# Two rows of w2 moved to the front of the down projection, in three transfers issued by GpSimd and one by SP

## The chip, the core and the metric

The kernel runs on one core of one Trainium2 chip. The metric is the device time of one execution in microseconds; lower is better. Three runs of the kernel before took 138.73, 138.76 and 138.94 us, so the median is 138.76 us. A profile shows one execution, whose span is counted from the first to the last instruction; what lies around the span belongs to the time as well.

## The reference

One decode step of a transformer block for a batch of 4, in bfloat16:

```
h   = x + attention(layernorm(x)) @ wo          # 32 heads, 4 kv heads, last 2048 keys
g   = layernorm(h) @ w1                         # [4,1024] @ [1024,3584]
u   = layernorm(h) @ w3
out = h + (silu(g) * u) @ w2                    # [4,3584] @ [3584,1024]
```

Some 55.6 MB of weights and caches are read once each: wq and wo (8 MB each), the windows of K and V (8 MB each), w1, w3 and w2 (7 MB each).

## The kernel before

**Storage.** One tile in SBUF, `ring`, has five units of 32 KB per partition. wq, K, V, wo, w1, w3 and w2 are laid into the units one after another, and each transfer waits until the readers of what it overwrites are done. w1 takes unit 1 and most of unit 2, w3 unit 3 and most of unit 4.

**w2.** It is cut into 128 partitions with 28 rows of 1024 values each (2 KB per row and partition), so partition p holds rows 28p to 28p+27. `W2B = [13, 8, 4, 2, 1]` gives the pieces: the first 13 rows of every partition go to the start of the ring (unit 0), the others one behind another to the start of unit 1, where w1 lies. The piece of 1 row is loaded as two halves (`h` in the loop at L509 to L512).

**Transfers.** `load` (L124) issues on the queue of SP. All the large transfers go through it, in the order of the code: wq in two pieces, K, V, wo, w1, w3, then w2 in pieces of 13, 8, 4, 2, 1/2 and 1/2 rows. In one queue the transfers of a DMA engine follow each other in order. x is loaded from the queue of ACT at the start. GpSimd issues no transfer.

**The stage around the change.** The order of the instructions is written out by hand (`manual_schedule`). After attention and the output projection, layernorm gives `hn_T`. `up_projection` (L489) multiplies it by w1 into `gate` (64 matmuls, in two halves of 8 steps of 4), ACT and DVE compute silu from it, and the second `up_projection` multiplies by w3 into `up`. DVE forms `hg` from both in two halves and transposes each into `hg_T` (L520, L218), which holds 28 columns of 32, one for each row of w2.

**The down projection** is in two forms. The first 21 rows, of the pieces 13 and 8 (`NE = 2`), are "early": two matmuls of 512 columns for each row, into `early_ps` (L538). DVE then adds `early_ps` to `h1`, the residual, in two steps of 64 partitions (L549). The other 7 rows, of the pieces 4, 2 and 1, are "late": six matmuls for each row (four of 128 columns, two of 256) into three tiles `y2_ps` (L554). Behind the piece of 4, one matmul with an identity (L565) adds a part of `h1` into `y2_ps[1]`. At the end ACT and DVE write `res` (L577 to L582) and SP and ACT issue four output transfers (L587).

On PE the order before is: up projection, early 13 rows, early 8 rows, late 4 rows, the `h1` matmul, late 2 rows, late 1 row. PE waits ahead of each piece for its transfer.

Of the kernel before, what the change touches and what calls it, by code (L numbers as in the profile page):

```python
# [10 lines left out]
P = 128  # L11
# [10 lines left out]
def kernel(  # L22
# [20 lines left out]
    nc = tc.nc  # L43

    B, _, D = A_x.shape
# [7 lines left out]
    FC = F // P  # L53
    NK = W // P
    C = 4
    R = 32
    S = R // B
    DQ = D // C
# [23 lines left out]
    w2_v = B_w2.rearrange("(p fc) n -> p fc n", fc=FC)  # L82
# [15 lines left out]
    def at(unit, *shape):  # L98
        o = unit * UNIT
        view = ring[:, o : o + int(np.prod(shape))]  # L100
        if len(shape) == 1:
            return view
        names = "abc"[: len(shape)]
        return view.rearrange(
            f"p ({' '.join(names)}) -> p {' '.join(names)}", **dict(zip(names, shape))
        )
# [4 lines left out]
    wo_s = at(3, T, D)  # L111
    w1_s = at(1, KC, F)
    w3_s = at(3, KC, F)
    W2B = [13, 8, 4, 2, 1]
    w2_s = []
    o = 0
    for i, n in enumerate(W2B):
        if i == 1:
            o = UNIT
# [3 lines left out]
    def load(dst, src):  # L123
        nc.sync.dma_start(out=dst, in_=src)  # L124
# [13 lines left out]
    for b in range(B):  # L138
# [10 lines left out]
    ident_f = const.tile([P, P], FP32)  # L149
# [8 lines left out]
        out=same[:], in_=t32[:].rearrange("p (o h) -> p o h", o=1).to_broadcast([P, C, R])  # L158
    )
    gmask = const.tile([P, 1, Hkv], BF16)  # L160
    with nc.allow_low_precision("sums of zeros and a single one"):
        nc.vector.tensor_reduce(
            out=gmask[:, 0], in_=t32[:].rearrange("p (g r) -> p g r", g=Hkv), axis=AX.X, op=ALU.add
# [3 lines left out]
    for j in range(JM):  # L167
# [3 lines left out]
        out=nscale[:], in_=ident_f[:2, :2], scalar=-qscale, op=ALU.mult  # L171
# [5 lines left out]
        out=place[:, : R * C].rearrange("p (h e) -> p h e", e=C)[:, :, C - 1], in_=t32[:]  # L177
# [6 lines left out]
        out=gather[:, :, :B], in_=ident[:].rearrange("p (c b s) -> p c b s", c=C, b=B)[:, :, :, 0]  # L184
# [44 lines left out]
    for kc in range(KC):  # L229
        for hf in range(2):  # L230
            for c in range(C):
                o = (2 * c + hf) * HALF * Dh
                nc.tensor.matmul(  # L233
                    q_ps[R * c : R * c + R, hf],
                    lhsT=xn_T[:, kc, :],
                    rhs=wq_s[:, kc, o : o + HALF * Dh],
                    start=(kc == 0),
                    stop=(kc == KC - 1),
                    tile_position=(0, R * c),
# [5 lines left out]
    for r in range(REP):  # L245
# [8 lines left out]
        out=Qm[:].rearrange("p b (g y) -> p b g y", y=QW)[:, :, :, :REP],  # L254
        in_=qT_ps[:, :, :, :B].rearrange("p r g b -> p b g r"),
# [184 lines left out]
    for e in range(C):  # L440
        nc.tensor.matmul(
            on_ps[:],
            lhsT=place[:, C - 1 - e : C - 1 - e + P],
            rhs=om[:, :, e * T : (e + 1) * T],
            start=(e == 0),
            stop=(e == C - 1),
# [6 lines left out]
    for i in range(2):  # L453
        for k in range(2):
            c = i + 2 * k
            nc.tensor.matmul(
                y_ps[R * i : R * i + R, k],
                lhsT=gather[:, c, :],
                rhs=x_nat[:],
                start=(k == 0),  # L460
                stop=False,
                tile_position=(0, R * i),
                skip_group_check=True,
            )
    for t in range(T):
        row = wo_s[:, t].rearrange("p (k i n) -> p i k n", k=2, i=2)
        for i in range(2):
            nc.tensor.matmul(  # L468
                y_ps[R * i : R * i + R],
                lhsT=oP[:, t, :],  # L470
                rhs=row[:, i],
                start=False,
                stop=(t == T - 1),
                tile_position=(0, R * i),
                skip_group_check=True,
            )
    load(w3_s, w3_v)
    load(w2_s[0], w2_v[:, : W2B[0], :])
    h1 = act.tile([P, DQ], FP32)
# [9 lines left out]
    def up_projection(w, out_ps):  # L489
        cols = w.rearrange("p k (c q h j) -> p k c h q j", c=C, h=2, j=FJ)  # L490
        for hf in range(2):
            for kc in range(KC):
                for c in range(C):
                    nc.tensor.matmul(  # L494
                        out_ps[hf][R * c : R * c + R, :],
                        lhsT=hn_T[:, kc, :],
                        rhs=cols[:, kc, c, hf],
                        start=(kc == 0),
                        stop=(kc == KC - 1),
                        tile_position=(0, R * c),  # L500
                    )
# [4 lines left out]
    hg = act.tile([P, 2, FH], BF16, tag="hg")  # L506
    up_projection(w1_s, [gate_ps[:, hf, :FH] for hf in range(2)])
    fc = W2B[0]
    for w, n in zip(w2_s[1:], W2B[1:]):  # L509
        for h in (slice(0, D),) if n > 1 else (slice(0, D // 2), slice(D // 2, D)):  # L510
            load(w[:, :, h], w2_v[:, fc : fc + n, h])
        fc += n  # L512
    nc.scalar.activation(out=eg[:], in_=gate_ps[:, :, :FH], func=ACT.Exp, scale=-1.0)
    nc.scalar.activation(out=eg[:], in_=eg[:], func=ACT.Identity, bias=1.0)  # L514
# [3 lines left out]
    hg_T = act.tile([P, FC, R], BF16)  # L518
    for hf in range(2):
# [5 lines left out]
    DH = DQ // 2  # L525
    y2_ps = [
        ps.tile(shape, FP32, tag=tag, name="y2_ps")
        for shape, tag in (([P, DH], "scA"), ([P, DH], "ktB"), ([P, DQ], "scB"))
    ]
    NE = 2  # L530
    FE = sum(W2B[:NE])

    fc = 0
    for w, n in zip(w2_s[:NE], W2B[:NE]):
        for ff in range(n):
            row = w[:, ff].rearrange("p (k i n) -> p i k n", k=2, i=2)
            for i in range(2):
                nc.tensor.matmul(  # L538
                    early_ps[R * i : R * i + R],
                    lhsT=hg_T[:, fc, :],  # L540
                    rhs=row[:, i],
                    start=(fc == 0),
                    stop=(fc == FE - 1),
                    tile_position=(0, R * i),
                )
            fc += 1
    for k in range(2):
        part = h1[2 * R * k : 2 * R * k + 2 * R, :]
        nc.vector.tensor_tensor(out=part, in0=early_ps[:, k], in1=part, op=ALU.add)  # L549
    for m, (w, n) in enumerate(zip(w2_s[NE:], W2B[NE:])):  # L550
        for ff in range(n):
            for t, c, size in ((0, 0, DH), (0, 1, DH), (1, 0, DH), (1, 1, DH), (2, 2, DQ), (2, 3, DQ)):
                o = c * DQ + t % 2 * DH
                nc.tensor.matmul(  # L554
                    y2_ps[t][R * c : R * c + R, :],
                    lhsT=hg_T[:, fc, :],
                    rhs=w[:, ff, o : o + size],
                    start=(fc == FE),
                    stop=(fc == FC - 1),
                    tile_position=(0, R * c),  # L560
                    skip_group_check=True,
                )
            fc += 1
        if m == 0:
            nc.tensor.matmul(  # L565
                y2_ps[1][: 2 * R, :],
                lhsT=ident_f[:, : 2 * R],
                rhs=h1[:, DH:],
                start=False,
                stop=False,  # L570
                skip_group_check=True,
            )
    res = act.tile([P, DQ], BF16)
    for k in range(2):
        part = slice(2 * R * k, 2 * R * k + 2 * R)
        if k == 0:
            nc.scalar.copy(out=res[part, DH:], in_=y2_ps[1][part, :])  # L577
            nc.vector.tensor_tensor(
                out=res[part, :DH], in0=y2_ps[0][part, :], in1=h1[part, :DH], op=ALU.add
            )  # L580
        else:
            nc.vector.tensor_tensor(  # L582
                out=res[part, :], in0=y2_ps[2][part, :], in1=h1[part, :], op=ALU.add
            )
        for i, eng in enumerate((nc.sync, nc.scalar)):
            c = 2 * k + i
            eng.dma_start(  # L587
                out=out_flat[:, c * DQ : (c + 1) * DQ], in_=res[R * c : R * c + B, :]
# [31 lines left out]
```

## Time and profile before

| | before |
|---|---|
| median of 3 runs | 138.76 us |
| the profiled execution's own time | 138.7 us |
| its span | 136.7 us |
| PE busy, DVE busy, ACT busy, POOL busy | 74.8, 49.9, 28.8, 15.3 us |
| read from HBM, mean rate over the span | 55.58 MB, 407 GB/s |
| last matmul of the gate ends | 104.1 us |
| up projection (w3) | 116.3 to 121.1 us |
| early matmuls of 13 rows, of 8 rows | 124.35 to 127.3, 129.15 to 131.05 us |
| last matmul ends | 133.95 us |

The page of the profile gives busy time by engine, the span in 40 slices, the DMA queues, and the chain that ended last. From the trace come, besides, the order in time of all instructions, and of every DMA packet its queue, start, duration and bytes. The packets do not name their DMA engine; but on an engine a packet starts as the one before it ends, so that the sixteen series ("lanes") can mostly be followed. Each transfer ends on each lane that it uses with a packet of 4 bytes, which signals its end. An instruction that waits for a transfer waits for the signals of all its lanes.

### The profile page before, as it was taken

How to read it: one execution, taken by the hardware profiler on the slowest of the kernel's cores; microseconds unless marked ns; L12 is line 12 of the kernel's file. 1: busy time of each engine (PE TensorE's matmuls, PEld its weight loads, DVE VectorE, ACT ScalarE, POOL GpSimd, SP SyncE). 2: the span in 40 equal slices, each digit the busy share in tenths (PEclk: the TensorE clock that was granted, in tenths of full speed). 3: DMA queues.
4: the chain of work that ended last, by engine and by line, in shares of the span. 5: the costliest groups of instructions: out<-in, count | busy, mean ns of one | idle time of the engine just before them, and what ended most of it. 6: DMA issues, size and time to landing. Idle time of an engine off the chain costs nothing.

```text
span 136.7 us, 1762 instructions
## 1 busy us (share of the span) xinstructions
PE 74.8 (55%) x762; PEld 40.6 (30%) x762; DVE 49.9 (37%) x50; ACT 28.8 (21%) x32; POOL 15.3 (11%) x41
## 2 busy tenths in 40 slices
PE   0000044959999986029966875994184000946471
PEld 0000011439957852014423323341042000413240
DVE  0000110006526363989799920004100594090022
ACT  3000130025968495104000000000405400000000
POOL 7300060000000000000176333000200000000000
PEclk9999999999999999955999999599959955599999
DMA  4999697999999999998978979969799798999960
GB/s 163 497 454 538 269 537 307 432 417 451 408 432 436 412 436 408 436 585 360 556 326 364 556 326 475 520 285 537 336 470 508 302 520 372 384 423 432 384 245 2
DMA packets 2795, 55.70 MB, mean 408 GB/s; under 512 B 324, under 2 KB 612, under 8 KB 740
## 3 DMA queue, kind: packets, MB, share of 16 engines
q1 hardware_dynamic: 2752, 55.58, 95.3%
q8 instruction: 6, 0.10, 0.3%
q10 hardware_dynamic: 36, 0.01, 0.0%
q14 instruction: 1, 0.01, 0.0%
HBM read 55.58 MB, written 0.01 MB: 407 GB/s over the span
## 4 chain that ended last, share of the span: by engine, by line
DMA 59%; PE 28%; DVE 6%; ACT 3%; SPq 1%; issue 1%; DVEq 0%
DMA ring<-in_B_w_dram 43%; DMA ring<-in_A_wq_dram 15%; PE kt_ps L267 9%; PE sc_ps L290 5%; PE q_ps L233 4%; PE o_ps L381 4%; PE gate L494 3%; DVE P L344 2%; DVE PT L366 2%; ACT ring L271 1%; PE small L381 1%; DVE ring L269 1%; SPq L124 1%; DVE rmax L302 1%; ACT q_sb L243 1%
## 5 line engine op out<-in xcount | busy, mean ns | idle before, releaser
L271 ACT COPY ring<-kt_ps 128x2048 bf16<-128x2048 bf16 x8 | 14.6, 1866 | 7.1 <-PE kt_ps L267 7.1
L267 PE MATMUL kt_ps<-ident,ring 128*128 128x128 bf16 x256 | 15.0, 219 | 0.6 <-DVE Qm L253 0.5
L267 PEld LDWEIGHTS <-ring 128*128 128x128 bf16 x256 | 14.4, 98 | 2.6 <-issue 2.6
L269 DVE COPY ring<-kt_ps 128x2048 bf16<-128x2048 bf16 x8 | 9.8, 1225 | 9.3 <-PE kt_ps L267 9.3
L398 POOL TENSOR_TENSOR o<-od 128x256 f32<-128x256 f32 x4 | 6.8, 1695 | 54.2 <-DVE od L389 54.2
L193 PE MATMUL sums_ps<-both,mean_f 128*128 128x64 f32 x4 | 1.1, 366 | 18.9 <-ACT both L191 18.9
L494 PE MATMUL up<-ring,n_T 128*32 128x448 bf16 x64 | 4.7, 467 | 12.2 <-DMA ring<-in_B_w_dram 12.2
L494 PEld LDWEIGHTS <-n_T 128*32 128x32 bf16 x128 | 4.2, 121 | 20.2 <-DMA ring<-in_B_w_dram 12.7
L344 DVE TENSOR_TENSOR P<-p,gmask 128x2048 bf16<-128x2048 bf16 x4 | 9.1, 2278 | 0.8 <-ACT p L331 0.8
L381 PEld LDWEIGHTS <-PT 128*128 128x128 bf16 x64 | 6.7, 107 | 9.0 <-issue 1.9
L366 DVE STREAM_TRANSPOSE PT<-P 128x2048 bf16<-128x2048 bf16 x4 | 9.2, 2306 | 0.1
L515 DVE RECIPROCAL eg<-eg 128x896 f32<-128x896 f32 x1 | 5.8, 5753 | 9.5 <-ACT eg L514 9.5
L468 PE MATMUL y_ps<-ring,oP 128*32 128x512 bf16 x64 | 8.8, 442 | 0.1
L233 PE MATMUL q_ps<-ring,n_T 128*32 128x512 bf16 x64 | 6.6, 587 | 3.8 <-DMA ring<-in_A_wq_dram 2.0
L381 PE MATMUL o_ps<-ring,PT 128*128 128x512 bf16 x32 | 8.6, 430 | 0.0
L290 PE MATMUL sc_ps<-ring,Qm 128*32 128x512 bf16 x64 | 7.6, 604 | 0.4 <-DVE ring L269 0.4
L538 PE MATMUL early_ps<-ring,hg_T 128*32 128x512 bf16 x42 | 4.9, 379 | 5.1 <-DMA ring<-in_B_w_dram 5.1
L381 PE MATMUL small<-ring,PT 128*128 128x512 bf16 x32 | 7.2, 379 | 0.7 <-DVE rinv L362 0.7
L193 PEld LDWEIGHTS sums_ps<-both,mean_f 128*128 128x128 f32 x4 | 0.8, 248 | 19.4 <-issue 16.9
L494 PE MATMUL gate<-ring,n_T 128*32 128x448 bf16 x64 | 4.6, 458 | 3.2 <-DMA ring<-in_B_w_dram 3.2
L577 ACT CAST res<-y_ps 64x128 bf16<-64x128 f32 x1 | 0.3, 259 | 26.3 <-PE y_ps L554 26.3
L218 DVE STREAM_TRANSPOSE x_T<-x_nat 128x256 bf16<-128x256 bf16 x1 | 0.6, 626 | 13.0 <-DMA x_nat<-in_A_x_dram 13.0
(81 smaller groups left out, 62.5 us busy)
## 6 DMA issues: line engine op xcount, KB each, us to landing
ring<-in_B_w_dram SPq DMA_DIRECT2D x2, 7168.0 KB
ring<-in_A_k_cache_dram SPq DMA_DIRECT2D x4, 2048.0 KB, 25.6
ring<-in_A_v_cache_dram SPq DMA_DIRECT2D x4, 2048.0 KB, 42.9
ring<-in_A_wq_dram SPq DMA_DIRECT2D x1, 7168.0 KB, 21.2
ring<-in_B_w_dram SPq DMA_DIRECT2D x1, 3328.0 KB
ring<-in_B_w_dram SPq DMA_DIRECT2D x1, 2048.0 KB
ring<-in_A_wq_dram SPq DMA_DIRECT2D x1, 1024.0 KB, 4.6
ring<-in_B_w_dram SPq DMA_DIRECT2D x1, 1024.0 KB, 28.1
```

The source lines that it names most:

```text
L233: nc.tensor.matmul(q_ps[R * c : R * c + R, hf], lhsT=xn_T[:, kc, :], rhs=wq_s[:, kc, o : o + HALF * Dh], start=(kc == 0), stop=(kc == KC - 1),
L267: nc.tensor.transpose(out=kt_ps[:, jj], in_=blocks[:, jj, :], identity=ident[:])
L269: nc.vector.tensor_copy(out=blocks, in_=kt_ps[:])
L271: nc.scalar.copy(out=blocks, in_=kt_ps[:])
L290: nc.tensor.matmul(sc_ps[b // 2][R * q : R * q + R, b % 2], lhsT=Qm[:, b, g * R : (g + 1) * R], rhs=kT[:, b, g, q], start=(g == 0), stop=( ...
L344: nc.vector.tensor_tensor(out=P4[:], in0=stage.pop(("p1", b))[:].rearrange("p (x o) -> p x o", o=1).to_broadcast([P, JR * L5, Hkv]), in1=g ...
L366: nc.vector.transpose(out=PT[:].rearrange("p j h -> p (j h)"), in_=stage.pop(("P4", b))[:].rearrange("p x g -> p (x g)"),)
L381: nc.tensor.matmul(o_ps, lhsT=PT[:, i * JM : (i + 1) * JM, :].rearrange("p j h -> p (j h)"), rhs=v_s[b][:, i * JM : (i + 1) * JM, :], star ...
L398: nc.gpsimd.tensor_tensor(out=o2[:], in0=od[:, :2], in1=od[:, 2:], op=ALU.add)
L468: nc.tensor.matmul(y_ps[R * i : R * i + R], lhsT=oP[:, t, :], rhs=row[:, i], start=False, stop=(t == T - 1), tile_position=(0, R * i), ski ...
L494: nc.tensor.matmul(out_ps[hf][R * c : R * c + R, :], lhsT=hn_T[:, kc, :], rhs=cols[:, kc, c, hf], start=(kc == 0), stop=(kc == KC - 1), ti ...
L515: nc.vector.reciprocal(out=eg[:], in_=eg[:])
```

## The change

`W2B` becomes `[13, 2, 8, 4, 1]`: rows 13 and 14 of every partition are now the second piece, at the start of unit 1. This piece is loaded by four transfers of whole partitions: GpSimd issues partitions 0 to 9, then 29 to 127, then 10 to 20 (`SPARE`), and SP partitions 21 to 28, between its pieces of 13 and of 8 rows. GpSimd's transfers wait only for those gate matmuls that read the first part of w1, and for earlier transfers; SP's queue then holds 13 rows, 8 partitions of 2 rows, 8 rows, 4 rows and two halves.

On PE the piece of 2 rows is worked first, in the late form (12 matmuls into `y2_ps`), then the early pieces of 13 and of 8 rows. The `h1` matmul now contracts over the 64 partitions that matter to its output, instead of all 128 of which the others met zeros. It thus waits only for DVE's first addition, and stands ahead of the late 4 rows and the last row. The counts of matmuls and bytes stay as they are.

```
-    W2B = [13, 8, 4, 2, 1]
+    W2B = [13, 2, 8, 4, 1]
+    SPARE = ((0, 10), (29, P), (10, 21))
...
-    for w, n in zip(w2_s[1:], W2B[1:]):
-        for h in (slice(0, D),) if n > 1 else (slice(0, D // 2), slice(D // 2, D)):
-            load(w[:, :, h], w2_v[:, fc : fc + n, h])
+    for i, (w, n) in enumerate(zip(w2_s[1:], W2B[1:]), 1):
+        if i == 1:
+            for a, b in SPARE:
+                nc.gpsimd.dma_start(out=w[a:b], in_=w2_v[a:b, fc : fc + n, :])
+            a, b = SPARE[2][1], SPARE[1][0]
+            load(w[a:b], w2_v[a:b, fc : fc + n, :])
+        else:
+            for h in (slice(0, D),) if n > 1 else (slice(0, D // 2), slice(D // 2, D)):
+                load(w[:, :, h], w2_v[:, fc : fc + n, h])
...
+    EARLY = (0, 2)
+    def late(m, ff, start=False, stop=False):
+        for t, c, size in ((0, 0, DH), (0, 1, DH), (1, 0, DH), (1, 1, DH), (2, 2, DQ), (2, 3, DQ)):
+            o = c * DQ + t % 2 * DH
+            nc.tensor.matmul(
+                y2_ps[t][R * c : R * c + R, :],
+                lhsT=hg_T[:, sum(W2B[:m]) + ff, :],
+                rhs=w2_s[m][:, ff, o : o + size],
+                start=start, stop=stop, tile_position=(0, R * c), skip_group_check=True,
+            )
+    for ff in range(W2B[1]):
+        late(1, ff, start=(ff == 0))
+    for m in EARLY:
+        for ff in range(W2B[m]):
...
...
     for k in range(2):
         part = h1[2 * R * k : 2 * R * k + 2 * R, :]
         nc.vector.tensor_tensor(out=part, in0=early_ps[:, k], in1=part, op=ALU.add)
...
+    nc.tensor.matmul(
+        y2_ps[1][: 2 * R, :],
+        lhsT=ident_f[: 2 * R, : 2 * R],
+        rhs=h1[: 2 * R, DH:],
+        start=False, stop=False, skip_group_check=True,
+    )
+    for m in (3, 4):
+        for ff in range(W2B[m]):
+            late(m, ff, stop=(m == 4))
```

More of the change, by code (lines that the diff above doesn't have):

```diff
@@ L529 @@
     ]
[L530 to L536, printed above, removed]
+    EARLY = (0, 2)
[6 more added lines that the diff above has]
+                rhs=w2_s[m][:, ff, o : o + size],
+                start=start,
+                stop=stop,
+                tile_position=(0, R * c),
+                skip_group_check=True,
+            )
[3 more added lines that the diff above has]
+        for ff in range(W2B[m]):
+            row = w2_s[m][:, ff].rearrange("p (k i n) -> p i k n", k=2, i=2)
             for i in range(2):
@@ L539 @@
                     early_ps[R * i : R * i + R],
-                    lhsT=hg_T[:, fc, :],
+                    lhsT=hg_T[:, sum(W2B[:m]) + ff, :],
                     rhs=row[:, i],
-                    start=(fc == 0),
-                    stop=(fc == FE - 1),
+                    start=(m == 0 and ff == 0),
+                    stop=(m == EARLY[-1] and ff == W2B[m] - 1),
                     tile_position=(0, R * i),
                 )
-            fc += 1
     for k in range(2):
@@ L549 @@
         nc.vector.tensor_tensor(out=part, in0=early_ps[:, k], in1=part, op=ALU.add)
[L550 to L572, printed above, removed]
+    nc.tensor.matmul(
+        y2_ps[1][: 2 * R, :],
+        lhsT=ident_f[: 2 * R, : 2 * R],
+        rhs=h1[: 2 * R, DH:],
+        start=False,
+        stop=False,
+        skip_group_check=True,
+    )
+    for m in (3, 4):
+        for ff in range(W2B[m]):
+            late(m, ff, stop=(m == 4))
     res = act.tile([P, DQ], BF16)
```

## The prediction

> **What bounds the kernel now.** I read the chain of waits first. Its last third is one piece, the stream of weights, and only 3.1 us of the 136.7 us span lie behind it. Columns: start, duration, what.
>
> ```profile
> 104.96 28.65 DMA ring<-in_B_w_dram
> 133.61 0.04 issue
> 133.65 0.30 PE y_ps L554 x2
> 133.97 0.43 DVE res L582
> ```
>
> The page's queue rows say that one queue fills the DMA engines, and that two others carry instructions.
>
> ```profile
> q1 hardware_dynamic: 2752, 55.58, 95.3%
> q8 instruction: 6, 0.10, 0.3%
> q14 instruction: 1, 0.01, 0.0%
> ```
>
> Then the windows of 1 us at the end (columns: window, length, PE, PEld, DVE, ACT, POOL, clock, DMA share, GB/s). The reader is to see that the 16 engines do not stop together: the share falls two microseconds before the last byte.
>
> ```profile
> 130.00:131.00 1.00, 1.00 (x10) 0.44 (x7) 0.00 (x0) 0.00 (x0) 0.00 (x0) 1.00 1.00 393
> 131.00:132.00 1.00, 0.39 (x20) 0.33 (x21) 0.83 (x2) 0.00 (x0) 0.00 (x0) 1.00 0.63 237
> 132.00:133.00 1.00, 0.72 (x24) 0.46 (x18) 0.00 (x0) 0.00 (x0) 0.00 (x0) 1.00 0.40 136
> 133.00:134.00 1.00, 0.88 (x18) 0.41 (x17) 0.31 (x2) 0.26 (x1) 0.00 (x0) 1.00 0.01 4
> ```
>
> Why, the trace's single DMA packets tell. On each engine (a lane, below) every transfer ends with a packet of 4 bytes, its signal. The signals of the 13 rows come at 121.85 to 122.32 on ten lanes, at 123.06 on one, and at 123.57 to 123.75 on five. For the 8 rows they are 126.75 to 127.22, 127.97, and 128.47 to 128.65; for the last half row 131.2 to 131.7, 132.43, and 132.93 to 133.12. The five arise one by one: each of the fetches of 16 KB of instructions on q8 (at 34.1, 40.7, 50.5, 82.5 and 105.6, about 1.05 us each) sets another lane back by some 1.5 us for good. The 8 KB on q14 at 119.12 sets the sixth back by 0.98. PE starts 0.49 us after the last signal (128.66 to 129.15; 133.13 to 133.61). So the five late lanes set the end.
>
> Last, the timeline of the tail, for what PE and DVE need behind each landing.
>
> ```profile
> 124.35 2.98 PE L538 MATMUL early_ps<-ring,hg_T 128*32 128x512 bf16 x26 [3.30 <-DMA ring<-in_B_w_dram]
> 129.15 1.90 PE L538 MATMUL early_ps<-ring,hg_T 128*32 128x512 bf16 x16 [1.82 <-DMA ring<-in_B_w_dram]
> 131.09 0.87 DVE L549 TENSOR_TENSOR h<-early_ps,h 64x256 f32<-64x256 f32 x2 [8.34 <-PE early_ps L538]
> 131.67 0.63 PE L554 MATMUL y_ps<-ring,hg_T 128*32 128x128 bf16 x24 [0.61 <-DMA ring<-in_B_w_dram]
> 132.23 0.43 PE L565 MATMUL y_ps<-h,ident_f 128*64 128x128 f32 x2
> ```
>
> **The change, part by part.** The bytes stay the same; the lanes and the order change. A packet of the two rows is 4 KB and takes 0.16 us (128 such packets in the trace, 159 to 172 ns). Before, each lane carries 8 of them behind the 4 rows.
>
> *How the 128 packets fall.* No row shows a transfer issued by GpSimd, so a lane's share lies between 0 and 12. The rows show that a transfer is cut evenly by a divisor of its outer size: 128 partitions give 16 signals, the 4 rows of an output 4, and x (16 partitions from 4 by 4 pieces) 4 signals with four packets each. Then 99 goes in nines over eleven lanes, 10 over ten, 11 over eleven, 8 over eight. I take them as filled in turn: 10 on lanes 0 to 9; 99 on 10 to 15 and 0 to 4; 11 on 5 to 15; SP's 8 on 0 to 7. That gives lanes 0 to 4 11 packets, 10 to 15 10, 5 to 7 3, and 8 and 9 2. Five lanes are spared, and five lag. That these are the same five I take from x: followed end to start, the four lanes that carry x lead, as far as ties allow, to none of the five.
>
> [...]
>
> *When they go.* GpSimd waits for the first third of a tile of w1, read by the 35th of the 64 gate matmuls, near 102; nothing else stands in its queue. Issue of one transfer: between 0.33 us (SP's shortest row) and 1.70 (POOL's longest mean, L398); three end between 103 and 107.1. I take the upper end, since POOL's own row is the nearer. Packets of two queues alternate: those of x went at 6.75, 8.89, 11.03 and 13.16, one per 57 KB packet of SP's. From 107.1 a lane has four turns in w3 (2.12 us each), then eight in the 13 rows (0.99 each), enough for ten packets by about 124, in either case before they are wanted. Cost here: nothing.
>
> *w3.* Late lanes take two packets more before its signal (115.84): +0.35 with the small signals. The up projection starts at 116.68; about half of that is made good, as less of it runs at the granted clock 0.5 (until 119.4). hg_T is ready at 122.9, off the path.
>
> *The head of the down projection.* It now needs the 13 rows and SP's 8 partitions: late lane 123.76 + 3 x 0.16 + 0.02 = 124.26, quick lane 122.32 + 1.75 = 124.07. PE starts at 124.26 + 0.49 = 124.75; 12 late matmuls at 0.63/24 each take 0.32, then the 26 early ones 2.98: done by 128.1. PE has idled 3.5 us before; the trace kept clock 1.00 over 3.3 us (121.05 to 124.35) and lost it by 109.2 after 104.1. If it were lost, 3.1 us at half speed (as from 116.3 to 119.4) would add 1.55: 129.6, still covered by the next landing.
>
> *The 8 rows* land at 128.66 + 0.49 = 129.15 on late lanes and 127.23 + 1.75 = 128.98 on quick ones; PE starts at 129.65, 0.50 later than now. This chain now sets the end, since the matmul that adds h1 stands ahead of the 4 rows in PE's queue and waits for DVE: 16 matmuls 1.90, to 131.55; step to DVE 0.04 and its first add 0.44 (half of 0.87), to 132.03; step and h1 matmul 0.03 + 0.43, to 132.49; 24 matmuls of the 4 rows 0.63, to 133.12; the last row 0.30, to 133.42. The halved contraction of the h1 matmul I cost at nothing: as many columns stream.
>
> *The last landing.* Late lanes lose 5 or 6 packets: 133.13 - 5 x 0.16 = 132.33; quick lanes gain 3: 131.7 + 0.48 = 132.18. PE could start the last row at 132.8; it is covered by the chain above. At most 0.3 us of the 0.8 won there is lost to that chain.
>
> Sum: the last matmul ends at 133.42 instead of 133.95, 0.53 us sooner. The profiled execution takes 138.7 us (span 136.7 and 2.0 around it), 0.06 under the median of 138.76. 138.7 - 0.53 = 138.17, so 138.2.
>
> **The rivals.** *One: the sixth late lane stays and is loaded.* If the q14 packet comes again and hits a lane with 10 or 11 packets, the 8 rows land there at 127.98 + 1.59 (or 1.75) = 129.57 (129.73), PE starts at 130.06 (130.22), and the chain of 3.77 us ends at 133.83 (133.99): 138.6 to 138.7, no change. For it: the packet is in this trace, and x's lanes may contain it. Against: no instruction starts with it, and nothing shows that it recurs.
>
> *Two, the other side: a late lane is among the loaded ones.* It then carries 10 or 11 packets ahead of the 8 rows: 128.66 + 1.59 to 1.75, + 0.49, + 3.77 = 134.5 to 134.67, or 139.25 to 139.4. It decides from the point where a late lane gets more than six of the packets (128.66 + 6.5 x 0.16 = 129.7, tying with now). So it is where the turn starts elsewhere, or where 99 is cut into sevens over fifteen lanes. [...] For it: no row says on which lane GpSimd begins. Against: the match of five and five.
>
> *Three: GpSimd costs more than I take.* The head needs all four pieces; if the last lands after 126.3, each further microsecond is one of the whole, as 12 and 26 matmuls (3.3 us) then end behind 129.65. A late issue or packets slower than 0.16 us would do it: 139 and up. Against: over 20 us for 0.5 MB.
>
> *Four: nothing is won, as the engines are shared.* The total of packets is unchanged, and if lanes lagged otherwise in most executions the spared ones would not matter: 138.7. The windows above speak against it. [...]
>
> **How the numbers follow.** Forecast as summed 0.42; rival one 0.18; two 0.22; three 0.12; four 0.06. The range: down to 138.0, if the clock or the queueing gives the chain another 0.2; up to 139.4, the upper end of two; about 2 in 10 are left out, mostly of three. Own range of the forecast: 138.0 to 138.4. A change of 0.2% (0.28 us) is about what a measurement of this kernel can tell. Faster: 0.38 of the forecast and 0.04 of one, 0.42. Same: 0.03, 0.12, 0.02 of two, 0.01 of three and 0.04 of four, 0.22. Slower: the rest, 0.36.
>
> **What the next profile would show.** Right: GpSimd issues before 107; the 12 late matmuls ahead of the early ones at about 124.8; the 16 early ones at 129.65; no wait for DMA ahead of the last row; the DMA share high until 132 and gone by 132.4. Rival one: the 16 start at 130.1, with one lane behind. Two: they start near 130.9 and the last signal comes after 133.5. Three: PE idles beyond 126 ahead of the late matmuls. The prediction is wrong if the fetches of instructions fall on other lanes than the spared ones.

## The result and the profile after

The changed kernel takes 142.38 us in the median of six runs (141.76 to 143.11); the kernel before took 138.70 us in six runs beside it. The ratio is 1.0266, with an interval of 1.0221 to 1.0310: 3.7 us slower, where 0.5 us faster was predicted. The profiled execution took 141.83 us, with a span of 139.9 (before: 138.7 and 136.7). The six runs alternate between about 141.8 and about 143.0; the profile is one of the lower ones.

First the queues of the changed kernel (packets, MB, share of 16 engines' span).

```profile
q1 hardware_dynamic: 2624, 55.09, 94.0%
q0 software_dynamic: 192, 0.49, 1.0%
```

The 0.49 MB are GpSimd's three transfers. They take 1.0% of the DMA engines' time: by this view they cost next to nothing. GpSimd issued them when the prediction had them issued, the third by 105.19 us:

```profile
103.34 1.85 POOL L513 DMA_DIRECT2D ring<-in_B_w_dram  x3 [6.15 <-PE gate L495]
```

The stretch in which they move beside SP's stream shows the loss. One window from 107 to 126 us (length, the engines' busy times, clock, DMA share, GB/s), first before, then after:

```profile
107.00:126.00 19.00, 6.36 (x80) 2.95 (x82) 9.96 (x6) 0.38 (x1) 0.00 (x0) 0.73 0.98 419
```

```profile
107.00:126.00 19.00, 4.90 (x64) 2.05 (x64) 10.11 (x6) 1.28 (x2) 0.00 (x0) 0.64 0.98 365
```

The DMA share is 0.98 in both. The engines are as busy as before, and move 365 GB/s instead of 419: the packets last longer. 19 us at 365 instead of 419 are 1.03 MB less, 2.5 us of the stream as it was. The trace's single packets say whose. GpSimd's own 4 KB packets took 0.159 to 0.22 us, all but three of the 120 (0.171 in the median), near the 0.16 that was predicted. SP's packets of 26 KB (one partition's 13 rows), which took 0.991 us in the median before, took 1.21, three quarters of them over 1.15, the longest 1.46; those of 57 KB (w3) that began after 107.3 took 2.36 us in the median and up to 2.57, against 2.12 before. On the lanes that do not lag, 7.92 us lay between the signal of w3 and that of the 13 rows; now about 10.7. GpSimd's packets account for less than half of that: seven of 0.16 are 1.1 us, and the lane that got no data packet at all from GpSimd still needed 9.77.

The timeline of PE shows what became of the head of the down projection.

```profile
117.95 4.90 PE L495 MATMUL up<-ring,n_T 128*32 128x448 bf16 x64 [12.92 <-DMA ring<-in_B_w_dram]
128.73 0.62 PE L542 MATMUL y_ps<-ring,hg_T 128*32 128x128 bf16 x12 [5.88 <-DMA ring<-in_B_w_dram]
129.11 6.10 PE L558 MATMUL early_ps<-ring,hg_T 128*32 128x512 bf16 x42
135.71 0.43 PE L569 MATMUL y_ps<-h,ident_f 64*64 64x128 f32 x2 [0.51 <-DVE h L568]
136.07 0.74 PE L542 MATMUL y_ps<-ring,hg_T 128*32 128x128 bf16 x30
```

PE waited 5.88 us for the first 13 rows and the pieces of the two rows. The 26 and the 16 early matmuls, which were apart before, are one group without a wait: the 8 rows had landed by the time PE got to them. The clock was 0.50 by then, as the windows show:

```profile
129.00:130.00 1.00, 1.00 (x17) 0.49 (x10) 0.00 (x0) 0.00 (x0) 0.00 (x0) 0.50 1.10 467
130.00:131.00 1.00, 1.00 (x8) 0.48 (x6) 0.00 (x0) 0.00 (x0) 0.00 (x0) 0.50 0.93 393
132.00:133.00 1.00, 1.00 (x12) 0.53 (x9) 0.00 (x0) 0.00 (x0) 0.00 (x0) 1.00 0.99 410
```

So the chain that ends last (start, duration, what) is no longer the stream to its end. From 128.73 it is work of PE and DVE:

```profile
103.06 25.53 DMA ring<-in_B_w_dram
128.59 0.14 issue
128.73 0.61 PE y_ps L542 x8
129.34 3.96 PE early_ps L558 x26
133.30 1.92 PE early_ps L558 x16
135.24 0.43 DVE h L568
135.67 0.04 issue
135.71 0.43 PE y_ps L569 x2
136.14 0.63 PE y_ps L542 x19
136.80 0.03 DVE res L585
```

The account, in PE's starts: the up projection 116.34 before, 117.95 now. The head comes at 128.73 instead of the 124.35 at which the 13 rows started before. The 12 and 26 matmuls take 4.57 us (0.61 + 3.96), against 3.30 at full clock. The last matmul ends at 136.8 instead of 133.95, 2.8 us later. The last 0.3 us is DVE's: the two additions into `res` now start at 136.80 and 137.11, one behind the other, since the 4 rows and the last row run as one burst of 30 matmuls; before, the first of them (133.57) ran while PE was still at work. 2.8 and 0.3 make the 3.1 us between 138.7 and 141.83.

The late head is not the whole reason. The stream itself ends as much later: the last signal of its last half row came at 135.93, where it had come at 133.13. With the 0.49 us to PE's start and the 0.30 of the last row, as before, that alone would end the last matmul near 136.7 (an estimate from these rows).

### The profile page after: what moved, and what is told of

Read it like the earlier page. It is cut to its first block, busy times and chain, and to the rows that moved or that the text cites. A ratio compares the mean times of both kernels' runs of the same rounds, so it can differ in the third digit from the quotient of the medians.

```text
span 139.9 us, 1769 instructions
## 1 busy us (share of the span) xinstructions
PE 77.0 (55%) x762; PEld 41.4 (30%) x762; DVE 50.1 (36%) x50; ACT 28.8 (21%) x32; POOL 17.1 (12%) x44
## 4 chain that ended last, share of the span: by engine, by line
DMA 55%; PE 33%; DVE 6%; ACT 3%; issue 1%; DVEq 0%; SPq 0%
DMA ring<-in_B_w_dram 40%; DMA ring<-in_A_wq_dram 15%; PE kt_ps L268 9%; PE sc_ps L291 5%; PE o_ps L382 4%; PE early_ps L558 4%; PE q_ps L234 3%; PE gate L495 3%; DVE P L345 2%; DVE PT L367 2%; ACT ring L272 1%; PE small L382 1%; PE y_ps L542 1%; DVE ring L270 1%; DVE rmax L303 1%
## 5 line engine op out<-in xcount | busy, mean ns | idle before, releaser
L382 PE MATMUL o_ps<-ring,PT 128*128 128x512 bf16 x32 | 11.3, 530 | 0.0
L382 PEld LDWEIGHTS <-PT 128*128 128x128 bf16 x64 | 7.5, 119 | 10.2 <-issue 5.4
L234 PE MATMUL q_ps<-ring,n_T 128*32 128x512 bf16 x64 | 5.9, 530 | 3.6 <-DMA ring<-in_A_wq_dram 1.9
L495 PE MATMUL gate<-ring,n_T 128*32 128x448 bf16 x64 | 5.6, 530 | 3.5 <-DMA ring<-in_B_w_dram 3.5
L469 PE MATMUL y_ps<-ring,oP 128*32 128x512 bf16 x64 | 7.1, 379 | 0.1
L558 PE MATMUL early_ps<-ring,hg_T 128*32 128x512 bf16 x42 | 6.1, 446 | 0.0
```

The lines of the kernel that those rows point to most:

```text
L234: nc.tensor.matmul(q_ps[R * c : R * c + R, hf], lhsT=xn_T[:, kc, :], rhs=wq_s[:, kc, o : o + HALF * Dh], start=(kc == 0), stop=(kc == KC - 1),
L382: nc.tensor.matmul(o_ps, lhsT=PT[:, i * JM : (i + 1) * JM, :].rearrange("p j h -> p (j h)"), rhs=v_s[b][:, i * JM : (i + 1) * JM, :], star ...
L469: nc.tensor.matmul(y_ps[R * i : R * i + R], lhsT=oP[:, t, :], rhs=row[:, i], start=False, stop=(t == T - 1), tile_position=(0, R * i), ski ...
L495: nc.tensor.matmul(out_ps[hf][R * c : R * c + R, :], lhsT=hn_T[:, kc, :], rhs=cols[:, kc, c, hf], start=(kc == 0), stop=(kc == KC - 1), ti ...
L558: nc.tensor.matmul(early_ps[R * i : R * i + R], lhsT=hg_T[:, sum(W2B[:m]) + ff, :], rhs=row[:, i], start=(m == 0 and ff == 0), stop=(m == ...
```

## The experiments

The first question was which part of the change is dear: the new order, GpSimd as the issuer, or the cut into 10, 99, 11 and 8 partitions. Where nothing else is said, times are medians, with the range of the runs, and the kernel before took 138.70 to 138.74 us beside them.

**The new order, without any second queue.** The changed kernel, but SP loads the two rows in one transfer of 128 partitions, between its pieces of 13 and of 8 rows.

```
-            for a, b in SPARE:
-                nc.gpsimd.dma_start(out=w[a:b], in_=w2_v[a:b, fc : fc + n, :])
-            a, b = SPARE[2][1], SPARE[1][0]
-            load(w[a:b], w2_v[a:b, fc : fc + n, :])
+            nc.sync.dma_start(out=w, in_=w2_v[:, fc : fc + n, :])
```

> The changed kernel, but its two rows come in one transfer of 128 partitions on SP's queue, between the 13 and the 8 rows; GpSimd issues nothing. Theory (each turn that GpSimd's queue takes on a DMA engine costs 0.2 us beyond the packet's own time): w3 lands as before (up projection at 116.3), the 8 rows 1.28 us later than before, last matmul near 134.2, time 138.9 to 139.0. Rival one (the new order of the pieces on PE costs): about 142, as the changed kernel. Rival two (the cut of 99 partitions over the lanes costs): 139.0, as the theory.

139.25 us (138.81 to 139.56), ratio 1.0036 [1.0022, 1.0049]. PE in its timeline:

```profile
130.40 1.90 PE L555 MATMUL early_ps<-ring,hg_T 128*32 128x512 bf16 x16 [0.23 <-DMA ring<-in_B_w_dram]
133.17 0.73 PE L539 MATMUL y_ps<-ring,hg_T 128*32 128x128 bf16 x30
```

The order is worth nothing. The two rows ahead of the 8 delay those (130.40 instead of 129.15), and the chain behind them, 3.50 us long, ends the last matmul at 133.90, where it ended before (133.95). The second addition into `res` starts at 134.21 instead of 133.97, for the reason given above, and these 0.24 us are the whole difference of the two profiled executions (138.94 and 138.7). The median lies another 0.3 above this profile. 3.1 us of the loss (142.38 less 139.25) are thus left for the transfers.

**The issuer.** The same with GpSimd, or ACT, issuing the one transfer (`nc.gpsimd` or `nc.scalar` in the last line).

> The changed kernel, but its two rows come in one transfer of 128 partitions issued by GpSimd: eight packets on every lane. Theory: eight data turns and a signal cost 1.3 us of bytes and some 1.8 us of turns ahead of the 8 rows; up projection at 117.3 or later, head of the down projection near 127.5 to 128, time near 140.8. Rival one: 142. Rival two: with the even cut the loss is gone, 139.0.

> The same as the run with one GpSimd transfer, but issued on ACT's queue. Theory, as far as it is of GpSimd's queue alone: no cost of turns, up projection at 117 or before, time near 139.0. If any second queue costs turns: 140.8 as with GpSimd. Rival one: 142.

139.19 us (138.99 to 140.19), ratio 1.0037 [1.0021, 1.0053] with GpSimd; 139.06 (138.95 to 140.22), 1.0037 [1.0017, 1.0056] with ACT. Whichever engine issues, it is the time of the order alone. GpSimd's window:

```profile
107.00:126.00 19.00, 6.51 (x78) 2.85 (x80) 10.09 (x6) 1.45 (x2) 0.00 (x0) 0.62 0.98 419
```

The rate is the old 419 GB/s, with 128 packets of GpSimd's (159 to 165 ns, all but one) beside SP's, whose 26 KB packets stay at 0.993 us. So a second queue beside the stream cost nothing by itself (139.19 us, against 139.25 without it), and my first theory, that each turn of GpSimd's queue costs a lane some 0.2 us, falls.

**Turns alone.** To the kernel before, one transfer by GpSimd into a tile that nothing reads:

```
+    spare = act.tile([P, 256], BF16, tag="spare")
+    nc.gpsimd.dma_start(out=spare[:], in_=w2_v[:, 0, :256])
```

> The kernel before, and besides one transfer issued by GpSimd of 512 bytes for each of 128 partitions, to a tile that nobody reads, issued near 97 us: eight packets of 27 ns on every lane. Theory: the turns cost 0.2 us each whatever their size, so the landings from the 13 rows on come some 1.8 us later, time near 140.5. Rivals one and two: only the bytes count, 0.2 us, 138.9.

139.09 us (139.03 to 139.37), 1.0028 [1.0017, 1.0038]. The expectation missed, and its premise too: the 128 pieces of 512 bytes went as 16 packets of 4 KB, not as 128. It adds only that this GpSimd transfer, 64 KB over all partitions, cost 0.4 us (139.09 less 138.70).

**The cut.** Four kernels keep the order and change how the two rows are cut: eight GpSimd transfers of 16 partitions; eight of all 128 partitions with an eighth of the columns each; two, of partitions 0 to 31 and 32 to 127; and the cut of the change on ACT's queue instead of GpSimd's.

```
+            for a in range(0, P, 16):
+                nc.gpsimd.dma_start(out=w[a : a + 16], in_=w2_v[a : a + 16, fc : fc + n, :])
```

> The changed kernel, but its two rows come in eight GpSimd transfers of 16 consecutive partitions: eight packets and eight signals on every lane, as even as one transfer of 128, but each transfer's sixteen lanes write into the same sixteen partitions. Theory now (partitions: in a transfer of 128 a lane keeps to its own eight partitions; a packet that goes to another lane's partitions slows that lane's stream and its own): the 26 KB packets of the 13 rows take 1.2 us instead of 0.99 as in the changed kernel, up projection near 118, time 142 or more. Rival (the uneven cut of 99 over fifteen lanes costs): even cut, 139.2 as with one transfer. Rival (the number of transfers and signals costs): slow too, 141 or more.

> The changed kernel, but its two rows come in eight GpSimd transfers of 128 partitions and 512 bytes each: eight signals and 64 packets on every lane, each lane in its own partitions. Theory of partitions: as one transfer, 139.2, with 26 KB packets at 0.99 us. Rival of the uneven cut: 139.2. Rival of transfers and signals: as slow as eight of 16 partitions, 141 or more.

> The changed kernel, but its two rows come in two GpSimd transfers, of partitions 0 to 31 and 32 to 127: two and six packets on every lane, none left out. Theory of partitions: most packets go to other lanes' partitions, 26 KB packets at 1.15 us or more, time 141 to 142. Rival of the uneven cut: 139.2. Rival of transfers and signals (two instead of three): 140 to 141.

> The changed kernel, its three transfers of 10, 99 and 11 partitions issued on ACT's queue instead of GpSimd's. Theory of partitions: it is not GpSimd's queue, so the 26 KB packets stretch here as well, time 141 to 143. Rival of the uneven cut: by a common divisor eleven lanes take 11 to 12 packets and five none, quick lanes later by 0.6, time 139.5 to 140. If it is GpSimd's way of cutting: 139.2.

| cut of the two rows | median (range), us | ratio to before [95%] | 26 KB packets, us |
|---|---|---|---|
| GpSimd, one of 128 partitions | 139.19 | 1.0037 | 0.993 |
| GpSimd, 8 times 16 partitions | 145.5 (145.07 to 145.9) | 1.0490 [1.0466, 1.0514] | 1.24 |
| GpSimd, 8 times 128 partitions, by columns | 141.38 (140.69 to 141.84) | 1.0204 [1.0179, 1.0230] | 1.04 |
| GpSimd, 32 and 96 partitions | 141.8 (141.21 to 142.57) | 1.0227 [1.0189, 1.0264] | 1.19 |
| ACT, the cut of the change | 142.99 (142.15 to 143.49) | 1.0303 [1.0266, 1.0340] | 1.18 |

The windows of the 16 partitions, of 32 and 96, and of ACT, in this order:

```profile
107.00:126.00 19.00, 5.25 (x64) 2.22 (x64) 10.09 (x6) 0.31 (x1) 0.06 (x1) 0.64 0.99 349
```

```profile
107.00:126.00 19.00, 5.99 (x76) 2.58 (x77) 10.10 (x6) 0.47 (x1) 0.00 (x0) 0.64 0.98 366
```

```profile
107.00:126.00 19.00, 4.80 (x64) 2.02 (x64) 10.04 (x6) 1.04 (x2) 0.00 (x0) 0.64 1.00 373
```

GpSimd is not needed for the loss, nor is an uneven cut: eight times 16 is even by its count (256 packets, 128 with data and 16 signals for each transfer) and dearest. Beside transfers of fewer than all partitions SP's packets of 26 KB took 1.18 to 1.24 us, beside one transfer of all partitions 0.993. The cut by columns missed its expectation of 139.2. Its packets hardly stretch (1.04 us); it loses elsewhere, because PE's head waits for the last of the eight transfers, until 127.25. The 42 early matmuls then take 6.40 us, against 4.88 before (2.98 and 1.90):

```profile
127.25 0.27 PE L543 MATMUL y_ps<-ring,hg_T 128*32 128x256 bf16 x1 [1.01 <-DMA ring<-in_B_w_dram]
127.25 6.40 PE L559 MATMUL early_ps<-ring,hg_T 128*32 128x512 bf16 x42
```

**The same bytes, with nobody waiting.** To set the wait aside, three kernels add to the kernel before 512 KB by GpSimd into a tile that nothing reads: in one transfer, eight of 16 partitions, or eight of an eighth of the columns. They work on the old order of PE.

```
+    spare = ktpool.tile([P, 2 * D], BF16, tag="P4")
+    rows = w2_v[:, 0:2, :].rearrange("p a n -> p (a n)")
+    for a in range(0, P, 16):
+        nc.gpsimd.dma_start(out=spare[a : a + 16, :], in_=rows[a : a + 16, :])
```

> The kernel before in its own order, and besides one GpSimd transfer of 128 partitions of 4 KB to a tile that nobody reads, issued near 97 us: the bytes of the two rows, added and aligned. Theory of partitions and all rivals: eight packets of 0.16 us on every lane, all later landings 1.28 us later, 140.0.

> The same added bytes in eight GpSimd transfers of 16 consecutive partitions; nothing else differs, and no matmul waits for them. Theory of partitions: besides the 1.28 us of bytes, three to five microseconds of stretched packets of w3 and the 13 rows, 143 to 145. If only the wait at the head of the down projection made the changed kernel slow: 140.0.

> The same added bytes in eight GpSimd transfers of 128 partitions and 512 bytes each. Theory of partitions: each lane in its own partitions, as with one transfer, 140.0 to 140.2. If the number of transfers, signals or packets makes the cost: as slow as eight of 16 partitions.

140.29 us (140.16 to 140.32) in one transfer, 1.0111 [1.0096, 1.0126]: the price of 512 KB more to move. 144.93 (144.41 to 145.39) in eight of 16 partitions, 1.0446 [1.0418, 1.0474]. 140.66 (140.6 to 140.75) in eight by columns, 1.0140 [1.0123, 1.0157], about 0.5 us above what was expected. Their windows, in this order:

```profile
107.00:126.00 19.00, 5.00 (x68) 2.24 (x70) 9.98 (x6) 1.06 (x2) 0.00 (x0) 0.64 0.97 412
```

```profile
107.00:126.00 19.00, 4.68 (x64) 2.02 (x64) 9.73 (x6) 0.39 (x1) 0.00 (x0) 0.64 0.96 334
```

```profile
107.00:126.00 19.00, 6.14 (x64) 2.35 (x64) 10.07 (x6) 0.55 (x1) 0.00 (x0) 0.64 0.97 403
```

The last two have the same bytes, the same 128 data packets of 4 KB, the same number of transfers and of signals (256 packets on GpSimd's queue in both). They differ in which partitions a transfer covers, and in nothing that PE waits for. One costs 4.3 us more than the other. Nor is it that a packet of 4 KB then goes to a single partition: the one transfer of 128 partitions has 128 such packets as well. That settles what is dear in the cut: it is the partitions, not the number of transfers or turns. GpSimd's queue (packets, MB, share) with 16 partitions each, then by columns:

```profile
q0 software_dynamic: 256, 0.52, 1.2%
```

```profile
q0 software_dynamic: 256, 0.52, 1.0%
```

**No second queue at all.** The changed kernel with all four pieces on SP's queue (`nc.gpsimd` becomes `nc.sync`).

> The changed kernel, with all four pieces of the two rows (10, 99, 11 and 8 partitions) on SP's queue, between the 13 and the 8 rows: no second queue. Theory of partitions: w3 and most of the 13 rows land as before (up projection at 116.3), the packets of the two rows and the first of the 8 rows stretch, 140.5 to 143. If two queues that alternate are needed for the loss: eleven lanes carry 12 packets instead of 8, 139.2 + 0.6 = 139.8.

143.35 us (143.12 to 143.59), 1.0333 [1.0318, 1.0349], 0.35 above the range expected. The cut is as dear on SP's own queue. Here the up projection keeps its time (116.30), and the 26 KB packets theirs (0.991): the pieces of the two rows come behind both. Those of the 8 rows (16 KB), beside which they pass, took over 1.06 us in a quarter of the cases (before: 0.614 in the median, 0.621 at most), and the head came at 129.12:

```profile
129.12 0.63 PE L542 MATMUL y_ps<-ring,hg_T 128*32 128x128 bf16 x12 [7.58 <-DMA ring<-in_B_w_dram]
```

**Source or destination, and which partitions.** My theory was now that a lane which writes into partitions that another lane's stream serves slows both; as the lane's own I took eight consecutive partitions, an assumption that no run shows. So: the spare 512 KB in eight transfers of every eighth partition (`spare[a::8, :]` from `rows[a::8, :]`); the same with 16 consecutive rows as the source; the reverse, every eighth row into 16 consecutive partitions; and the changed kernel's two rows by every eighth partition.

> The kernel before and the 512 KB more of the three spare kernels, again in eight GpSimd transfers of 16 partitions each, but each takes every eighth partition instead of 16 consecutive ones. Number of transfers, of packets (4 KB) and of bytes are those of the eight consecutive ones (144.93 us). If the lanes are filled in turn, lane i now writes only into the partitions 8i to 8i+7, which its own packets of SP's stream serve too. Theory A (a packet is slow, and slows others, where a lane writes into partitions that another lane's stream serves): as the one transfer of 128 partitions, 140.3 to 140.8; SP's packets of 26 KB at 0.99 to 1.05 us, mean rate above 405 GB/s. Theory B (a transfer of fewer than all partitions costs this by itself, wherever they lie): 144.9, packets of 26 KB at 1.31 us, rate 340 GB/s.

> As the eight transfers of every eighth partition, but each reads 16 consecutive rows of w2, as the consecutive kernel did; only the destination is by lanes. What lands in the spare tile is read by nothing. Theory A, destination side (SBUF): 140.3 to 140.8. Theory A, source side (the order in which a transfer reads w2): 144.9. Theory B: 144.9.

> The reverse: each of the eight transfers writes 16 consecutive partitions and reads every eighth row of w2. The spare tile is read by nothing. Theory A, destination side: as the consecutive kernel, 144.9, packets of 26 KB near 1.3 us. Source side: 140.3 to 140.8. Theory B: 144.9.

> The changed kernel's order, with its two rows of w2 in eight GpSimd transfers of every eighth partition; with 16 consecutive partitions each the same took 145.5 us, with one transfer of 128 partitions 139.19. Theory A: 139.2 to 139.8, up projection from about 117.1, 16 early matmuls near 130.5. Theory B: 145.5.

| destination of each transfer | source of each transfer | median (range), us | ratio [95%] | 26 KB packets, us | GB/s, 107 to 126 us |
|---|---|---|---|---|---|
| 16 consecutive | 16 consecutive | 144.93 (144.41 to 145.39) | 1.0446 [1.0418, 1.0474] | 1.31 | 334 |
| 16 consecutive | every eighth | 144.61 (144.15 to 145.01) | 1.0425 [1.0400, 1.0450] | 1.35 | 326 |
| every eighth | every eighth | 142.47 (142.29 to 143.05) | 1.0279 [1.0256, 1.0302] | 1.17 | 360 |
| every eighth | 16 consecutive | 142.66 (142.49 to 143.17) | 1.0290 [1.0263, 1.0316] | 1.15 | 360 |
| all 128, by columns | all 128 | 140.66 (140.6 to 140.75) | 1.0140 [1.0123, 1.0157] | 1.05 | 403 |

What is read, and in which order, makes no difference: rows one and two of the table agree within their ranges, and so do three and four. The destination makes 2.1 to 2.3 us between them. So this part of the loss is on the side of the destination, in SBUF; the other 1.8 us, between every eighth partition and all 128 by columns, these runs do not divide between source and destination. But every eighth partition was to cost nothing, and cost about half (142.47 us, between 140.66 and 144.93): neither "a transfer of few partitions costs so much" nor my theory with eight consecutive partitions fits.

The fourth run is not readable as a time. It took 148.72 us (147.88 to 149.91, ratio 1.0729 [1.0673, 1.0785]), but its up projection starts only at 129.72, although w3's last signal came at 116.74. It seems to wait for GpSimd's transfers, which it does not need (the last packet of theirs ended at 129.02); why, the trace does not show. In the kernel with 16 partitions each the up projection started at 118.52. Its 26 KB packets were 1.15 us, as those of the other two kernels with every eighth partition.

```profile
129.72 4.54 PE L495 MATMUL up<-ring,n_T 128*32 128x448 bf16 x64 [24.27 <-DMA ring<-in_B_w_dram]
```

**Own lane or foreign lane.** Two kernels were to tell whether it counts which lane writes into which partitions, with transfers of 8 partitions four apart, in pairs below and above partition 64. I took it that in the first kernel each lane writes into partitions that its own packets of SP's stream serve, and in the second, with each pair swapped, into those of another lane. No run shows that; it was my assumption. If it held, and a foreign lane is what slows, the first was to take 140.3 to 141.0 us, near the 140.29 of the one transfer, and the second 142.5 to 145.

```
+    for a in range(0, 64, 32):
+        for c in range(a, a + 4):
+            for p in (c, c + 64):
+                nc.gpsimd.dma_start(out=spare[p : p + 29 : 4, :], in_=rows[p : p + 29 : 4, :])
```

> The kernel before and the same 512 KB once more, in sixteen GpSimd transfers of 8 partitions each, taken four apart: c, c+4, ... c+28 and then c+64, c+68, ... c+92, for c = 0 to 3 and 32 to 35. So far the same bytes took 140.29 us in one transfer, 140.66 in eight of all partitions, 142.47 in eight of every eighth partition, 144.6 to 144.9 in eight of 16 consecutive ones; the order in which the source is read made no difference. [...] Theory B (transfers of few partitions are dear by themselves): twice as many transfers as the eight, so no better than 142.5 and rather 145. [...]

> As the kernel with sixteen transfers of 8 partitions four apart, with the two transfers of each pair swapped, so that the lanes that served partitions below 64 now write to those above, and the reverse. [...] If a foreign lane is enough to slow both: 142.5 to 145, packets of 26 KB above 1.1 us. [...]

142.44 us (142.14 to 142.71), 1.0269 [1.0253, 1.0285], and 142.24 (141.8 to 142.73), 1.0244 [1.0216, 1.0272]. The first is not near 140.3 to 141.0, the second not above 142.5, and they differ by 0.2 us; this is no answer, because the design failed. GpSimd's queue has 512 packets in each: 128 with data and 384 of 4 bytes, 24 for each transfer. 16 of these are signals, and 8 make up the count of 16 beside the 8 with data. So each transfer is dealt to all sixteen lanes, beginning, as this count can best be read, on the same one each time. The packets of the first kernel, followed end to start from 100.7 to 107 us, agree: eight lanes take a data packet of both transfers of a pair, and the other eight only small ones. So eight lanes got 16 data packets each, and the two kernels are nearly one. Eight packets more on a lane are 1.3 us at 0.16 each. With these the 140.29 us of the one transfer would be 141.6; what is left is too little to argue from. SP's packets do say one thing: those of 26 KB took 1.00 and 1.07 us in the median, less than the 1.15 to 1.35 of the four kernels that move the same spare 512 KB with 16 partitions in a transfer. So here transfers of few partitions did not stretch them by the same amount wherever these lay, though GpSimd also issued these transfers more slowly.

## Why the prediction was wrong

*What bounds the kernel.* That the stream sets the end stands. That its five late lanes do, and that to relieve them would win 0.5 us, was not tested: no run had lanes relieved without a cut into parts of the partitions, and with that cut every lane became later than the late ones had been: the first of the sixteen signals of the 13 rows came at 124.75, where the last had come at 123.76.

*How the 128 packets fall.* Wrong for GpSimd. "99 goes in nines over eleven lanes" is what ACT's queue did with the same cut (120 data packets and 32 signals: 10, 11 and 11). GpSimd's queue held 120 data packets and 72 of 4 bytes: three times 16 signals, and 24 to fill 10 up to 16, 99 to 112 and 11 to 16. So the 99 went in sevens over fourteen lanes and one on a fifteenth, the sevens of rival two. That the lanes are filled in turn, each transfer going on where the one before stopped, was my assumption, and no run shows it; the sixteen transfers of 8 partitions are best read as beginning on the same lane each time. The late lanes were not spared: as far as the packets can be followed, four of the five carried 7 to 9 data packets and one a single one. By rival two's sum, with 7 to 9 in place of 10 or 11, that would have been 138.8 to 139.1. It doesn't explain 142.4, and of the two kernels with partitions cut evenly over the lanes one lost more (145.5) and one nearly as much (141.8).

*When they go; "Cost here: nothing".* This is the step that failed. The issue (103 to 107.1) and the price of a packet (0.16 us) were right, and the sum took that price as the whole: a packet costs its own duration, on its own lane. The runs show a second term, which the trace of before could not hold, as all its large transfers cover all partitions: SP's 26 KB packets grew from 0.991 to 1.21 us, and to 1.20 on the lane that carried none of GpSimd's data. I bounded the number of packets on a lane, and the time of issue, but not the effect on the other queue's packets; the nearest row, the packets of x beside those of 57 KB, I read for their turns alone.

*w3.* +0.35 was predicted; the up projection started 1.62 us later. GpSimd's first data packet went at 107.60, beside w3, so the stretching began there. By the packets' own records the last signal of w3 came at 117.30, 1.45 later than before. The gap from that signal to PE's start was 0.49 us before and 0.65 here, and 0.94 in the changed order with eight transfers of 16 partitions, so that across runs I compare PE's starts, and packets with packets.

*The head of the down projection.* 124.75 was predicted; 128.73 came. Of the 3.98 us, 1.3 is w3's (1.62 less 0.35), the rest is in the 13 rows and SP's 8 partitions behind them: the last signal of these came at 127.83, where 124.26 was summed. GpSimd's own last signal had come at 126.29; PE did not wait for it.

*The clock.* The prediction had the case of a lost clock, 1.55 us, covered by the next landing. The clock was lost, for 1.27 us on these 38 matmuls, but the cover was gone, as the head began four microseconds late.

*The chain behind the 8 rows.* Right, and 0.3 too long: 3.77 us were summed, 3.50 measured with SP's transfer (130.40 to 133.90) and 3.47 in the changed kernel (133.30 to 136.77); the last 30 matmuls took 0.74 in one burst, where 0.93 was summed. The `h1` matmul, costed as unchanged, took 0.43 us with half the contraction (135.71) as with all of it (132.23 before). What the sum left out is DVE: its additions into `res` fall in one place now, +0.24 to +0.3 behind the last matmul.

*The last landing.* Right in that PE shows no wait for DMA ahead of the last row. But it was covered by little: the last signal came at 135.93, and PE came to the last six matmuls near 136.7. It came 2.8 us later than before, where the prediction had it come 0.8 earlier.

*The rivals.* One, the sixth lane: its 8 KB packet recurs in the profile of every run, between 119.1 and 120.95, so that the doubt about it was unfounded; what it costs cannot be seen under the loss. Three is the nearest: "packets slower than 0.16 us", and its sign of PE idle beyond 126 ahead of the late matmuls (it idled to 128.73). But it looked for the slow packets on GpSimd's queue, and they were on SP's; it gave this too little chance, 0.12, and the range ended below it. Four said that the sum of packets was unchanged. So it is in bytes; the rate at which they go is not.

What is shown: the new order brings nothing (139.25, +0.5 us); the cut into parts of the partitions brings the other 3.1 us, whichever queue carries it (142.38, 142.99 and 143.35 us on GpSimd's, ACT's and SP's); the number of transfers, the issuer and the source's order do not; about half of what 16 consecutive partitions cost over all 128 by columns (2.1 to 2.3 of 4.3 us) is on the side of the destination, in SBUF. What was only argued: that a lane slows another, and itself, where it writes into partitions that the other's stream serves, and that this is how the changed kernel's own cut loses. Left open: which partitions a lane serves, whether a foreign lane is what slows, and why the changed kernel alternates between 141.8 and 143.0 us. No run was faster than the kernel before, and none points to a version that would be: every kernel with a cut into parts of the partitions took 141.8 us or more in the median.

## What to carry to other kernels

Where a stream keeps all DMA engines busy (a share of 0.98 here), price an added transfer not by its bytes alone but by what it does to the stream's packets, and let every transfer cover all 128 partitions, also where only some are urgent. Split such a transfer by columns rather than by partitions: the same 512 KB added cost 1.6 us in one piece, 2.0 in eight by columns, and 6.2 in eight by 16 partitions. Best is not to split it: in the changed order one transfer took 139.19 us and eight by columns 141.38, as PE then waited for the eighth. A DMA share that stays at 0.98 while the GB/s fall (419 to 365 here) is the sign: read the two columns together, and then the duration of one size of packet before and after.

## What the runs showed of the hardware that was not expected

- Transfers of few partitions slowed the packets of another transfer: from 0.991 to between 1.15 and 1.35 us for 26 KB, from 419 to between 326 and 378 GB/s, where transfers of 10 to 99 partitions passed beside them on a second queue; with 8 partitions four apart, to 1.00 and 1.07 us, 394 and 392 GB/s. Between 16 consecutive partitions and every eighth, the destination counted and the source did not.
- GpSimd's transfers of 10, 99 and 11 partitions were filled up with packets of 4 bytes to 16, 112 and 16 (24 in all, beside 48 signals), those of 32 and 96 were not (160 packets: 128 with data, 32 signals); ACT's queue cut the same 99 over eleven lanes without filling (32 signals for the three transfers).
- GpSimd's transfer of 128 by 512 bytes went as 16 packets of 4 KB.
- One GpSimd transfer of 128 packets beside the full stream left the rate at 419 GB/s in the changed order; with 512 KB more to move it was 412.
- With sixteen transfers GpSimd issued eight (from 96.21 us) and then waited before each further one (the ninth at 104.61) for an earlier one to land.
- The gap from w3's last signal to PE's start was 0.48 to 0.52 us where nothing, or one transfer of 128 partitions, passed beside it, and 0.63 to 1.07 where two or more transfers did, by columns too (0.73 and 0.77).
